# A fused dense-GELU forward and backward on one core: b2 of the first block by GpSimd, more waking products, one joined group of left-over products

## The chip, the cores and the metric

One core of a Trainium2 chip. The metric is the device time of one launch in microseconds (us). The engines are TensorE (PE in the profile: products, with PEld its weight loads), VectorE (DVE), ScalarE (ACT), GpSimd (POOL) and SyncE (SP, which here only issues DMAs).

## The reference

The forward pass of a dense layer with a tanh-approximated GELU, and its gradients for an incoming `grad_out`:

```python
def _fwd_reference(x, w1, b1, w2, b2):
    h = jnp.einsum("bsd,df->bsf", x, w1) + b1
    h = _gelu(h)
    return jnp.einsum("bsf,fd->bsd", h, w2) + b2
_out, _vjp = jax.vjp(_f, x, w1, b1, w2, b2)
_grads = _vjp(grad_out)
return (_out0, *[jnp.asarray(_g) for _g in _grads])
```

B = 1, S = 2048 rows, D = 448, F = 1792, everything bf16. Six outputs: out (out_0), and the gradients of x, w1, b1, w2 and b2 (out_1 to out_5).

## The kernel before

**Stages.** The rows are cut into four blocks of 512 (`SB`), F into 14 tiles of 128, taken in 7 pairs per block, so 28 pairs in all. For pair `f` of a block, TensorE forms u = x w1 (`pe_u_fulls`, `u_tail`), and for pair `k` q = grad_out w2^T (`pe_q_fulls`, `q_tail`). ScalarE copies u out with b1 added (`copy_u`), and makes gelu(u) (`act_gelu`, into hT), a square and a tanh; VectorE makes from those the derivative of the gelu (`dve_cubic`, `dve_gate`) and multiplies it with q (`dve_gh`, line 299, into ghT). From hT come the rows of out (a `Unit` of kind "o": 128 rows, 14 products with w2_sb), from ghT the rows of the gradient of x (kind "x", with w1T_sb). After all pairs follow the gradients of w1 (`gw1_full`, `gw1_tail`), of w2 (`gw2_tile`) and of the biases (`emit_sum`).

**Left-over products.** D = 448 is three tiles of 128 and a left-over of 64. The products of the three full tiles are the "fulls" (lines 212 and 258). The left-over has only 64 rows, half the array; `pe_tails(fs, ks)` issues those of u (line 227) and of q (line 234) in turn, u's in one half of the array and q's in the other, so that a u and a q run at the same time when both lists are given.

**Order.** The order of the instructions on every engine is written out by hand (`manual_schedule`); the waits between engines are added for the data and the buffers. The sequence in question is the start, lines 395 to 424: u of pair 0, copy, square, gelu; u of pair 1; u of pair 2 and its left-over; four units of block 0 are opened and given their first pair of products (`pieces(4, 0, -1)`); left-over and fulls of q of pair 0; the gate and gh of pair 0; another `pieces`. Then a loop over i = 1 to 7: u of pair i + 2, joined left-overs of u and q, q of pair i, tanh, the finished units' evictions around `copy_u`, gelu and square, VectorE's chain, and pieces of the open units. At i = 6 two units of kind "x" are opened, the first readers of w1T_sb. From pair 8 on, two pairs go through at a time. PSUM has four single banks (tags one0 to one3), which u and units share, and two double ones (two0, two1); up to q 7 all q's use two0, so the next q waits until gh has read the one before.

**Loads.** All first loads but one of w1's pieces are issued from SP one after another in the order of use: x in two transposing halves, pieces of w1 (w_f, with the left-over rows in wt), w2 (w_sb), grad_out transposed (gT), w2 transposed in pieces (w2T), b2 spread over the partitions (b_bc in the profile), x of the second block, the last of w2T, w1 transposed whole (w1T_sb), and grad_out of the second block. While x is on its way, TensorE runs 32 products of zeros, the waking products (line 172).

**Evictions.** A finished unit is copied from PSUM into one of five staging buffers (`st`) and stored by a DMA issued from GpSimd (line 342). Kind "x" is copied by ScalarE (line 339), kind "o" by VectorE, which adds b2 in the same instruction (line 341). The four "o" units of block 0 are an exception: b2 is added by a 15th product per unit, of `row0` (ones in its first row, zeros elsewhere) with b2_bc (line 332), and ScalarE copies them. In the last stages the same five `st` buffers hold the results of `gw1_full`, `gw1_tail` and `gw2_tile`; `gb2_w`, the row sum of grad_out, has a buffer of its own.

**Names.** The profile leaves numbers and some suffixes out of names: U, A, Z are U4, A4, Z4; row is row0; b_bc is b2_bc; w_sb is w2_sb.

Of the kernel before, what the change touches and what calls it, by code (L numbers as in the profile page):

```python
# [10 lines left out]
ALU = mybir.AluOpType  # L11
BF16 = mybir.dt.bfloat16
F32 = mybir.dt.float32
# [6 lines left out]
def kernel(  # L20
# [15 lines left out]
    nc = tc.nc  # L36
    P = 128
    B, S, D = x.shape
# [6 lines left out]
    SB = 512  # L45
    NB = S // SB
    SPB = SB // P
    NPAIR = NF // 2
    NSTEP = NB * NPAIR
    NSINGLE = 8  # L50
    LEAD = 2
    NWAKE = 32
    STG = 5
    ROW0 = [SB, 2 * SB, 3 * SB, 0]
    WIDE = (0, 1)
# [8 lines left out]
    const = ctx.enter_context(tc.tile_pool(name="const", bufs=1))  # L64
# [4 lines left out]
    stg = ctx.enter_context(tc.tile_pool(name="stg", bufs=STG))  # L69
# [6 lines left out]
    b1_t16 = const.tile([P, 32], BF16, name="b1_t16")  # L76
    b1T = const.tile([P, NF], F32, name="b1T")
    b2_bc = const.tile([P, D], BF16, name="b2_bc")
    row0 = const.tile([P, P], BF16, name="row0")
    w1_f = const.tile([P, KF, F], BF16, name="w1_f")  # L80
    w2T = const.tile([P, KF + 1, F], BF16, name="w2T")
    wt1 = const.tile([P, F], BF16, name="wt1")
# [9 lines left out]
    def two_banks(n, name):  # L92
        return psum.tile([P, 2, SB], F32, name=name, tag=f"two{n}")
# [40 lines left out]

    nc.vector.memset(zero[:], 0.0)
    nc.gpsimd.memset(b1_rows[:], 0.0)
    nc.vector.memset(row0[:], 0.0)
    nc.vector.memset(row0[0:1, :], 1.0)
    nc.gpsimd.dma_start(out=b1_rows[0:NF, :], in_=b1.rearrange("(ft p) -> ft p", p=P))
    xT[0] = blk.tile([P, KF + 1, SB], BF16, name="xT", tag="xT")  # L140
    halves = [slice(0, SB // 2), slice(SB // 2, SB)]
# [28 lines left out]
    pw = two_banks(1, "pw")  # L170
    for w in range(NWAKE):
        nc.tensor.matmul(pw[:, 0, 0:P], lhsT=zero[:], rhs=zero[:], start=True, stop=True)
# [30 lines left out]
    def pe_u_fulls(f):  # L203
        b, p = divmod(f, NPAIR)
        if p == 0:
            hT[b] = blk.tile([P, NF, SB], BF16, name="hT", tag="hT")
        banks = (2, 3) if f == 1 else (0, 1) if f < NSINGLE + LEAD else order_a[2 * (f % 2):2 * (f % 2) + 2]
        PU[f] = [one_bank(n, "pu") for n in banks]
        for rs in halves if f == 0 else [slice(0, SB)]:
            for a in range(2):  # L210
                for kt in range(KF):
                    nc.tensor.matmul(PU[f][a][:, rs], lhsT=w1_f[:, kt, cols(p, a)], rhs=xT[b][:, kt, rs],  # L212
                                     start=(kt == 0 and rs.start == 0), stop=False, skip_group_check=True)
# [4 lines left out]
    def open_q(k):  # L218
        b, p = divmod(k, NPAIR)
        if p == 0:  # L220
            ghT[b] = blk.tile([P, NF, SB], BF16, name="ghT", tag="ghT")
        PQ[k] = two_banks(0 if k < NSINGLE else order_b[k % 2], "pq")

    def u_tail(f, a):
        b, p = divmod(f, NPAIR)
        hf = half(b not in WIDE)
        nc.tensor.matmul(PU[f][a][:], lhsT=wt1[hf, cols(p, a)], rhs=xT[b][hf, KF, :], start=False, stop=True,  # L227
                         tile_position=(hf.start, 0), skip_group_check=True)

    def q_tail(k, a, swap=False):  # L230
        b, p = divmod(k, NPAIR)
        hf = half((b in WIDE) != swap)
        g = g_swap[b] if swap else gT[b][:, 0, :]
        nc.tensor.matmul(PQ[k][:, a, :], lhsT=w2T[hf, 0, cols(p, a)], rhs=g[hf, :], start=True, stop=False,  # L234
                         tile_position=(hf.start, 0), skip_group_check=True)

    def pe_tails(fs, ks):
        cross = bool(fs) and bool(ks) and (fs[0] // NPAIR in WIDE) != (ks[0] // NPAIR in WIDE)
        for k in ks:
            open_q(k)  # L240
        us = [(f, a) for f in fs for a in range(2)]
        qs = [(k, a) for k in ks for a in range(2)]
        if not us and len(ks) == 2:
            for a in range(2):
                q_tail(ks[0], a)
                q_tail(ks[1], a, swap=True)
            return
        for n in range(max(len(us), len(qs))):
            if n < len(us):
                u_tail(*us[n])  # L250
            if n < len(qs):
                q_tail(*qs[n], swap=cross)

    def pe_q_fulls(k):
        b, p = divmod(k, NPAIR)
        for a in range(2):
            for kt in range(1, KF + 1):
                nc.tensor.matmul(PQ[k][:, a, :], lhsT=w2T[:, kt, cols(p, a)], rhs=gT[b][:, kt, :], start=False, stop=(kt == KF),  # L258
                                 skip_group_check=True)
# [55 lines left out]
    class Unit:  # L315
        def __init__(self, kind, b, j):
            self.kind, self.b, self.j, self.done, self.ps = kind, b, j, 0, None
            self.b2_pe = kind == "o" and b == 0
            self.by_act = kind == "x" or self.b2_pe

        def avail(self, fmax, gmax):
            top = fmax if self.kind == "o" else gmax
# [2 lines left out]
        def emit(self, p):  # L325
            src, w = (hT, w2_sb) if self.kind == "o" else (ghT, w1T_sb)
            for a in range(2):
                nc.tensor.matmul(self.ps, lhsT=src[self.b][:, 2 * p + a, self.j * P:(self.j + 1) * P],  # L328
                                 rhs=w[:, 2 * FP[p] + a, :], start=(p == 0 and a == 0),
                                 stop=(p == NPAIR - 1 and a == 1 and not self.b2_pe), skip_group_check=True)  # L330
            if p == NPAIR - 1 and self.b2_pe:
                nc.tensor.matmul(self.ps, lhsT=row0[:], rhs=b2_bc[:], start=False, stop=True, skip_group_check=True)  # L332
            self.done += 1

        def evict(self):
            st = stg.tile([P, SB], BF16, name="st", tag="st")
            r = ROW0[self.b] + self.j * P
            if self.by_act:
                nc.scalar.copy(out=st[:, 0:D], in_=self.ps)  # L339
            else:  # L340
                nc.vector.tensor_tensor(out=st[:, 0:D], in0=self.ps, in1=b2_bc[:], op=ALU.add)
            nc.gpsimd.dma_start(out=(out2 if self.kind == "o" else gx2)[r:r + P, :], in_=st[:, 0:D])  # L342
# [16 lines left out]
    def open_two(n, units):  # L359
        t = two_banks(n, "ps")  # L360
        for h in range(units):
            open_unit(t[:, h, 0:D])

    def pieces(budget, fmax, gmax):
        for un in list(open_units):
            while un.done < un.avail(fmax, gmax) and budget > 0:
                un.emit(un.done)
                budget -= 1
            if un.done == NPAIR:
                open_units.remove(un)  # L370
                finished.append(un)
# [36 lines left out]
    act_square([1])  # L408
    act_gelu([1])
    pe_u_fulls(2)  # L410
    pe_tails([2], [])
    open_two(1, 2)
    for n in (2, 3):
        open_unit(one_bank(n, "ps")[:, 0:D])
    pieces(4, 0, -1)
    pe_tails([], [0])
    pe_q_fulls(0)
    dve_gate([0])
    dve_cubic([1])
# [86 lines left out]
    accg = blk.tile([P, D], F32, name="accg", tag="ghT")  # L506
# [30 lines left out]
    def emit_sum(n):  # L537
        for _ in range(n):
            if not sums:
                return  # L540
            kind, st_ = sums.pop(0)
            if kind == "g":
                in0 = g_nat[:, 0, :] if st_ == 1 else accg[:]
                nc.vector.tensor_tensor(out=accg[:], in0=in0, in1=g_nat[:, st_, :], op=ALU.add)
                if st_ == NS - 1:
                    gb2_w = stg.tile([P, D], BF16, name="gb2_w", tag="gb2", bufs=1)
                    nc.gpsimd.partition_all_reduce(gb2_w[:], accg[:], channels=P, reduce_op=bass_isa.ReduceOp.add)
                    nc.gpsimd.dma_start(out=out_5.rearrange("(o d) -> o d", o=1), in_=gb2_w[0:1, :])
            else:
                v = acc[:].rearrange("p (ft f) -> p ft f", f=P)  # L550
                b, j = PLACE[st_]
                in0 = gh_nat[:, PLACE[0][0], :, PLACE[0][1], :] if st_ == 1 else v
                nc.vector.tensor_tensor(out=v, in0=in0, in1=gh_nat[:, b, :, j, :], op=ALU.add)  # L553
                if st_ == NS - 1:
                    gb1_w = blk.tile([P, F], BF16, name="gb1_w", tag="ghT")
                    for c in range(4):
                        c0, c1 = c * 512, min(F, c * 512 + 512)
                        nc.gpsimd.partition_all_reduce(gb1_w[:, c0:c1], acc[:, c0:c1], channels=P, reduce_op=bass_isa.ReduceOp.add)
                    v1 = out_3.rearrange("(o f) -> o f", o=1)
                    nc.gpsimd.dma_start(out=v1[:, 2 * P:F], in_=gb1_w[0:1, 0:F - 2 * P])  # L560
                    nc.gpsimd.dma_start(out=v1[:, 0:2 * P], in_=gb1_w[0:1, F - 2 * P:F])
# [43 lines left out]
    for ft0, n in ((0, 4), (4, 4), (8, 4), (12, 2)):  # L605
        for kt in range(KF):
            gw1_full(ft0, n, kt)
            emit_sum(3)
        if ft0 == 4:
            gw1_tail(0, 4)  # L610
        if ft0 == 12:
            gw1_tail(8, 3)
# [35 lines left out]
```

## Time and profile before

| what | us |
|---|---|
| runs | 272.23, 274.29, 273.76 (median 273.76) |
| profiled execution | 273.81 |
| its span, first to last instruction | 272.0 |

| engine | busy us | share of the span |
|---|---|---|
| PE (TensorE) | 267.1 | 98% |
| DVE (VectorE) | 175.7 | 65% |
| ACT (ScalarE) | 139.4 | 51% |
| POOL (GpSimd) | 38.2 | 14% |

How to read the views: the page's slices cut the span into 40 parts of 6.8 us, and each digit is the busy share of a part in tenths. The chain of waits follows the work that ended last back from the last instruction; in order of time, each line is a start, a length and what it was, with xN for N instructions in a row. A product's time in the chain is what it adds to the one before. The timeline has a start, a length (from the first start to the last end of a group), engine, line, operation, tiles written and read, shape and count; SPq, ACTq and POOLq are the engines' issues of DMAs. A line of the DMA issues ends with the size or the number, and the us from issue to landing. All times count from the first instruction of the span.

### The profile page before, as it was taken

The page shows a single profiled execution, that of the slowest core. Times are in us where ns is not written, and L with a number is a line of the kernel's source. Part 1 is how long each engine was busy: PE and PEld are TensorE (multiplying, and loading weights), DVE is VectorE, ACT ScalarE, POOL GpSimd, SP SyncE. Part 2 cuts the span into 40 slices and gives each one's busy share as a digit, 9 for nine tenths or more (in the row PEclk, how much of TensorE's full clock was granted, in tenths as well). Part 3 has the DMA queues.
Part 4 walks back from the last instruction along what each step waited for, and adds up shares of the span by engine and source line. Part 5 has one row for each costly group of instructions (what it writes and reads, how often), then busy time and mean ns, then how long its engine had stood idle before and what let it go on. Part 6 is the DMA issues. An engine that isn't in the chain of part 4 may idle for free.

```text
span 272.0 us, 3706 instructions
## 1 busy us (share of the span) xinstructions
PE 267.1 (98%) x1434; PEld 129.6 (48%) x1434; DVE 175.7 (65%) x208; ACT 139.4 (51%) x163; POOL 38.2 (14%) x50
## 2 busy tenths in 40 slices
PE   7999999999999999999999999999999999999995
PEld 6334344444444445444454455554444485555554
DVE  1488999999989799685979931109999992000000
ACT  2699899799994678768668610011111121112111
POOL 1000003111001001010110102120520007900000
PEclk9999999999999999999999999999999999999999
DMA  7999989999999966194352549999111111999861
GB/s 164 221 200 216 184 171 189 289 250 199 260 225 241 236 171 154 34 190 83 106 115 85 111 97 289 378 215 217 39 40 38 41 39 31 194 225 222 206 125 34
DMA packets 112961, 44.37 MB, mean 163 GB/s; under 512 B 92032, under 2 KB 111824, under 8 KB 112944
## 3 DMA queue, kind: packets, MB, share of 16 engines
q1 hardware_dynamic: 106352, 36.43, 63.4%
q0 software_dynamic: 1824, 4.27, 4.9%
q10 hardware_dynamic: 4768, 3.44, 4.0%
q8 instruction: 11, 0.18, 0.3%
q14 instruction: 6, 0.05, 0.0%
HBM read 7.23 MB, written 14.23 MB: 79 GB/s over the span
## 4 chain that ended last, share of the span: by engine, by line
PE 97%; DMA 2%; ACT 0%; issue 0%
PE ps L328 31%; PE ps_v L599 16%; PE pq L258 14%; PE pu L212 14%; PE ps_w L567 13%; PE pu L227 5%; PE ps_w L578 2%; DMA xT<-in_x_dram 2%; PE pq L234 1%; PE ps L332 0%; ACT st L602 0%
## 5 line engine op out<-in xcount | busy, mean ns | idle before, releaser
L328 PE MATMUL ps<-w_sb,hT 128*128 128x448 bf16 x224 | 44.8, 352 | 0.0
L328 PE MATMUL ps<-w1T_sb,ghT 128*128 128x448 bf16 x224 | 43.8, 352 | 0.0
L267 ACT ACTIVATE U<-pu,b1T 128x512 bf16<-128x512 f32 x55 | 33.8, 686 | 19.2 <-PE pu L227 19.0
L599 PE MATMUL ps_v<-g_nat,h_nat 128*128 128x448 bf16 (+1 forms) x240 | 42.6, 340 | 0.0
L212 PE MATMUL pu<-xT,w_f 128*128 128x512 bf16 (+1 forms) x174 | 40.8, 383 | 0.8 <-DMA xT<-in_x_dram 0.8
L342 POOL DMA_DIRECT2D out_dram<-st x32 | 17.6, 551 | 163.4 <-ACT st L339 108.4
L258 PE MATMUL pq<-gT,w2T 128*128 128x512 bf16 x168 | 39.4, 380 | 0.0
L299 DVE SCALAR_TENSOR_TENSOR ghT<-Z,pq 128x1024 bf16<-128x1024 bf16 x28 | 33.8, 1220 | 7.6 <-PE pq L258 5.9
L567 PE MATMUL ps_w<-gh_nat,x_nat 128*128 128x512 bf16 (+1 forms) x192 | 36.7, 352 | 0.0
L285 ACT ACTIVATE Z<-Z 128x2048 bf16<-128x2048 bf16 (+1 forms) x18 | 27.5, 1528 | 10.2 <-DVE Z L281 9.9
L599 PEld LDWEIGHTS <-h_nat 128*128 128x128 bf16 x240 | 23.3, 98 | 19.3 <-issue 0.3
L328 PEld LDWEIGHTS <-hT 128*128 128x128 bf16 x224 | 21.8, 98 | 21.2 <-ACT U L267 0.4
L328 PEld LDWEIGHTS <-ghT 128*128 128x128 bf16 x224 | 21.9, 98 | 20.9
L553 DVE TENSOR_TENSOR acc<-acc,gh_nat 128x1792 f32<-128x1792 f32 x14 | 30.0, 2142 | 0.5
L276 ACT ACTIVATE A<-U 128x1024 bf16<-128x1024 bf16 (+1 forms) x19 | 27.7, 1456 | 0.9 <-DVE U L269 0.6
L273 ACT ACTIVATE hT<-U 128x1024 bf16<-128x1024 bf16 (+1 forms) x20 | 27.7, 1390 | 0.2
L212 PEld LDWEIGHTS <-w_f 128*128 128x128 bf16 x174 | 17.5, 101 | 20.8 <-issue 2.5
L567 PEld LDWEIGHTS <-x_nat 128*128 128x128 bf16 x192 | 18.7, 98 | 17.9 <-issue 0.4
L258 PEld LDWEIGHTS <-w2T 128*128 128x128 bf16 x168 | 15.0, 98 | 23.2 <-issue 7.6
L602 ACT CAST st<-ps_v 128x448 bf16<-128x448 f32 (+1 forms) x15 | 7.6, 507 | 34.8 <-PE ps_v L599 34.8
L339 ACT CAST st<-ps 128x448 bf16<-128x448 f32 x20 | 10.3, 529 | 27.7 <-PE ps L328 27.5
L570 ACT CAST st<-ps_w 128x512 bf16<-128x512 f32 (+1 forms) x12 | 6.4, 532 | 29.9 <-PE ps_w L567 29.9
(46 smaller groups left out, 197.3 us busy)
## 6 DMA issues: line engine op xcount, KB each, us to landing
hT_dram<-hT SPq DMA_DIRECT2D x28, 256.0 KB, 3.4
out_dram<-st POOLq DMA_DIRECT2D x32, 112.0 KB, 3.3
x_nat<-in_x_dram SPq DMA_DIRECT2D x1, 1792.0 KB, 11.3
g_nat<-in_grad_out_dram SPq DMA_DIRECT2D x1, 1792.0 KB, 16.4
out_dram<-st ACTq DMA_DIRECT2D x13, 112.0 KB, 3.4
w_f<-in_w_dram SPq DMA_DIRECT2D x6, 192.0 KB, 3.7
out_dram<-st ACTq DMA_DIRECT2D x9, 128.0 KB, 1.7
w_sb<-in_w_dram SPq DMA_DIRECT2D x5, 224.0 KB, 3.5
```

Of the source, the lines that this page charges most:

```text
L212: nc.tensor.matmul(PU[f][a][:, rs], lhsT=w1_f[:, kt, cols(p, a)], rhs=xT[b][:, kt, rs], start=(kt == 0 and rs.start == 0), stop=False, ski ...
L258: nc.tensor.matmul(PQ[k][:, a, :], lhsT=w2T[:, kt, cols(p, a)], rhs=gT[b][:, kt, :], start=False, stop=(kt == KF), skip_group_check=True)
L267: nc.scalar.activation(out=dst, in_=PU[f][a][:], func=ACT.Identity, bias=bias)
L273: nc.scalar.activation(out=rows(hT, r), in_=part(U4, r), func=ACT.Gelu_apprx_tanh)
L276: nc.scalar.activation(out=part(A4, ks), in_=part(U4, ks), func=ACT.Square, scale=math.sqrt(3.0 * GELU_A * GELU_C))
L285: nc.scalar.activation(out=z, in_=z, func=ACT.Tanh, scale=-1.0 / 3.0)
L299: nc.vector.scalar_tensor_tensor(out=rows(ghT, [k]), in0=part(Z4, [k]), scalar=1.0, in1=PQ[k][:], op0=ALU.add, op1=ALU.mult)
L328: nc.tensor.matmul(self.ps, lhsT=src[self.b][:, 2 * p + a, self.j * P:(self.j + 1) * P], rhs=w[:, 2 * FP[p] + a, :], start=(p == 0 and a = ...
L342: nc.gpsimd.dma_start(out=(out2 if self.kind == "o" else gx2)[r:r + P, :], in_=st[:, 0:D])
L553: nc.vector.tensor_tensor(out=v, in0=in0, in1=gh_nat[:, b, :, j, :], op=ALU.add)
L567: nc.tensor.matmul(ps[:, 0:n * P], lhsT=x_nat[:, st_, kt * P:(kt + 1) * P], rhs=gh_nat[:, b, ft0:ft0 + n, j, :], start=(st_ == 0), stop=(s ...
L599: nc.tensor.matmul(ps[:, 0:w], lhsT=h_nat[ft][:, st_, :], rhs=g_nat[:, st_, h * w:(h + 1) * w], start=(st_ == 0), stop=(st_ == NS - 1))
```

## The change

There are five edits. The number of waking products goes from 32 to 42. The four "o" units of block 0 lose their 15th product, and `row0` with its two clears goes; ScalarE copies such a unit into a new f32 buffer `wide_st` (two of them), and GpSimd adds b2_bc to it on the way into `st`, ahead of the store that it issues. The left-over products of the third u (pair 2) are no longer issued by themselves behind its fulls: they are joined with those of the first q, behind `pieces(4, 0, -1)`. `gb2_w` takes one of the five `st` buffers in place of its own.

```diff
-    NWAKE = 32
+    NWAKE = 42
...
-    row0 = const.tile([P, P], BF16, name="row0")
...
-    nc.vector.memset(row0[:], 0.0)
-    nc.vector.memset(row0[0:1, :], 1.0)
...
-            self.b2_pe = kind == "o" and b == 0
-            self.by_act = kind == "x" or self.b2_pe
+            self.b2_later = kind == "o" and b == 0
+            self.by_act = kind == "x" or self.b2_later
...
-                                 stop=(p == NPAIR - 1 and a == 1 and not self.b2_pe), skip_group_check=True)
-            if p == NPAIR - 1 and self.b2_pe:
-                nc.tensor.matmul(self.ps, lhsT=row0[:], rhs=b2_bc[:], start=False, stop=True, skip_group_check=True)
+                                 stop=(p == NPAIR - 1 and a == 1), skip_group_check=True)
...
-                nc.scalar.copy(out=st[:, 0:D], in_=self.ps)
+                if self.b2_later:
+                    wide_st = stg.tile([P, D], F32, name="wide_st", tag="wide_st", bufs=2)
+                    nc.scalar.copy(out=wide_st[:], in_=self.ps)
+                    nc.gpsimd.tensor_tensor(out=st[:, 0:D], in0=wide_st[:], in1=b2_bc[:], op=ALU.add)
+                else:
+                    nc.scalar.copy(out=st[:, 0:D], in_=self.ps)
...
     act_gelu([1])
     pe_u_fulls(2)
-    pe_tails([2], [])
     open_two(1, 2)
     for n in (2, 3):
         open_unit(one_bank(n, "ps")[:, 0:D])
     pieces(4, 0, -1)
-    pe_tails([], [0])
+    pe_tails([2], [0])
     pe_q_fulls(0)
...
-                    gb2_w = stg.tile([P, D], BF16, name="gb2_w", tag="gb2", bufs=1)
-                    nc.gpsimd.partition_all_reduce(gb2_w[:], accg[:], channels=P, reduce_op=bass_isa.ReduceOp.add)
+                    gb2_w = stg.tile([P, SB], BF16, name="st", tag="st")[:, 0:D]
+                    nc.gpsimd.partition_all_reduce(gb2_w, accg[:], channels=P, reduce_op=bass_isa.ReduceOp.add)
```

## The prediction

> **What bounds the kernel now.** The profile's page first, engines and slices:
>
> ```profile
> PE 267.1 (98%) x1434; PEld 129.6 (48%) x1434; DVE 175.7 (65%) x208; ACT 139.4 (51%) x163; POOL 38.2 (14%) x50
> PE   7999999999999999999999999999999999999995
> DVE  1488999999989799685979931109999992000000
> ```
>
> TensorE is busy from the first slice to the last, so any TensorE time that goes away counts, unless something else then makes it wait. VectorE is nearly full in slices 3 to 11 (14 to 75 us): there the second limit lies. All edits but one fall before 49 us. The chain of waits, in order of time, prices the start:
>
> ```profile
> 0.72 4.63 DMA xT<-in_x_dram
> 5.40 2.72 PE pu L212 x12
> 8.12 0.96 PE pu L227 x2
> 9.08 1.55 PE pu L212 x6
> 10.63 0.54 PE pu L227 x2
> 11.17 1.40 PE pu L212 x6
> 12.57 0.54 PE pu L227 x2
> 13.11 1.62 PE ps L328 x8
> 14.72 0.54 PE pq L234 x2
> ...
> 16.66 1.51 PE ps L328 x8
> 18.17 1.30 PE pu L212 x6
> ...
> 41.00 0.19 PE ps L332
> ```
>
> The first pair of left-over products took 0.96, later pairs 0.54; the first 12 half-width products 2.72, though six of full width take 1.30 to 1.40. So TensorE ran at about half pace until some 0.3 us into the piece at 9.08, about 9.4. Groups just behind left-over products take 0.11 more (1.62 against 1.51, 1.40 against 1.30). Last, the timeline and the DMA issues of 34 to 50 us:
>
> ```profile
> 34.73 6.35 SPq L167 DMA_TRANSPOSE w1T_sb<-in_w_dram  x1
> 37.36 1.22 DVE L299 SCALAR_TENSOR_TENSOR ghT<-Z,pq 128x1024 bf16<-128x1024 bf16 x1
> 38.64 0.37 PE L234 MATMUL pq<-gT,w2T 64*128 64x512 bf16 x1
> 42.54 1.22 DVE L299 SCALAR_TENSOR_TENSOR ghT<-Z,pq 128x1024 bf16<-128x1024 bf16 x1
> 45.97 2.81 PE L328 MATMUL ps<-w1T_sb,ghT 128*128 128x448 bf16 x14
> 47.72 1.22 DVE L299 SCALAR_TENSOR_TENSOR ghT<-Z,pq 128x1024 bf16<-128x1024 bf16 x1
> ```
>
> ```profile
> w1T_sb<-in_w_dram SPq DMA_TRANSPOSE x1, 10.6
> ```
>
> These carry the forecast. The load of w1T_sb lands at 34.73 + 10.6 = 45.33, and its first reader starts at 45.97. SP issues its loads one behind another and none of them waits for TensorE, so this landing does not come earlier when TensorE does.
>
> **Waking products.** The 32 of before run from 0.98 to 4.58, a row of 3.60, so (3.60 - 0.31)/31 = 0.106 apart (0.31 is one's length). Ten more add 1.06: the last starts at 5.32, x lands at 0.72 + 4.63 = 5.35, and the 0.83 us of idle before the first product is filled. Bounds: if they change nothing, the first product starts up to 0.1 later. If the unbroken work needed for full pace is what the trace shows, 5.40 to 9.4 (4.0 us), it is reached at 0.98 + 4.0 = 5.0, and the 4.0 us at half pace shrink by 2.0. I take 1.6, nearer the second: loads behind it hold TensorE too, the first q's w2T at 13.1 (issued at 9.32, 3.8 to landing; used at 14.66) and the third q's at 22.6 (15.38, 7.2; used at 24.15), margins of 1.6 and 1.5. ScalarE and VectorE begin on the first u and so shift with it.
>
> **Left-over products of the third u beside the first q's.** One group goes: its 0.54 and the 0.11 behind it, 0.65. The remaining group costs what joined groups already cost (19.47 to 20.01, 0.54). What the move delays is ScalarE's copy of the third u, at 15.86: TensorE would finish it at 12.57 + 8 x 0.19 + 0.54 = 14.63, so 1.2 us hide it; beyond them ScalarE and the gelu behind it are late one for one. VectorE idled 0.38 before the first gh, waiting for q, so of the 0.65 it can follow by 0.38.
>
> **b2 off TensorE.** Four products of 0.19: 0.76, between 41.0 and 42.9. The removed clears of row0 (VectorE at 0.88 and 1.07) end long before its next work at 5.18: nothing.
>
> **b2 on GpSimd.** Four adds of 128x448. ScalarE's copy keeps its row (0.53, 128x448 from PSUM); writing f32 in place of bf16 is bounded by 0.51 and 0.62, the shortest such copy and VectorE's eviction of that shape; I take 0.53, and the ends make 4 x 0.09 = 0.4 at most on an engine that idles 0.9 at 49.5. For the add the trace has two bounds: VectorE's running sum of the same shape and operand types (14 in 9.20, 0.66 each), and GpSimd's own all-reduce of that shape (4.58). I take 0.66, the same arithmetic, and keep the other for the range. Behind each add on GpSimd's queue stand its store and, behind the fourth, the two copies at 47.59 and 48.14, whose first reader is the mixed left-over group at 75: 20 us of cover. The third copy needs wide_st back: it starts at 45.70 and the first add can start at 43.5, so an add up to 2.2 us long makes nobody wait; a longer one holds ScalarE and the gelu, square and tanh behind it.
>
> Here the trace shows no instruction of GpSimd's arithmetic beside VectorE, so the price to VectorE lies between 0 and the whole adds. The slack first: the gh that the eighth q waits for ends at 48.94, the q's first product starts at 50.01. With VectorE 1.6 earlier and TensorE 0.6, that is 1.07 + 1.0 = 2.07. Three adds lie before that gh: 3 x 0.66 = 1.98, just hidden even if VectorE stands still for all of it. The Trainium skill, SBUF — State Buffer, "Who interferes with whom", speaks against the change: a GpSimd instruction that reads SBUF and a VectorE one with two SBUF inputs exclude each other for a whole instruction. No run here shows it yet. By its companion GPSIMD Engine Reference, section 3.1 (4497 ns for 2048 elements), an add would be 0.98, an estimate, and three would leave TensorE 0.9 late, 274.1 in all.
>
> **gb2_w in the st ring.** It is read by its store, issued at 198.52 and landed 2.1 later. The fifth later st copy, which gets its slot, starts at 218.45: 17.8 us of cover, cost nothing. Were it gone, ScalarE's copies and the two ps_w banks would wait for that landing.
>
> **The sum.** Removed before 45.97: 1.6 + 0.65 + 0.76 = 3.0 us of TensorE. It can't all be kept. VectorE's gh end at 38.58 (37.36 + 1.22) and 43.76; the sixth q already waited for the first (started at 38.64), and the seventh starts at 44.12, 0.36 behind the second. VectorE moves by 1.6, or by 0.38 if the pace stays; so TensorE reaches the seventh q at most 1.6 + 0.36 = 2.0 earlier (or 0.38 + 0.36 = 0.74). Either is more than what w1T_sb leaves: 45.97 - 45.33 = 0.64, less 0.05 from landing to start (5.35 to 5.40 for x), **0.6**. Behind it TensorE never waits in the trace of before, so 0.6 stays to the end. The profiled execution took 273.81 (span 272.0, 1.8 around it; the median is 273.76): 273.81 - 0.6 = **273.2**.
>
> **The rivals.**
> 1. *The load is no wall.* Outside a profile, or by chance, it lands earlier. For: one run of before took 272.23, 1.6 less than the profiled one, which a fixed landing would not allow from an early start alone. Against: landings of this queue keep to its issue times. Next in line is the second block's gT, 41.12 + 7.3 = 48.4 against its use at 50.01: 1.6. Time 273.8 - 1.6 = 272.2; chance 0.25.
> 2. *VectorE is held by the adds* (slower). It decides from 2.07/3 = 0.69 per add; the 0.6 is used up at 0.89. At twice VectorE's row (1.32) the eighth q waits 3.96 - 2.07 = 1.9: 275.1. For: VectorE has no idle time there. Against: the gh instructions (1.22 each) read q from PSUM and could cover some of it. Chance 0.17.
> 3. *The waking products don't raise the pace.* The sum above shows that this changes nothing at the end: TensorE is 0.74 ahead instead of 2.0, and the wall leaves 0.6. It is inside the forecast.
>
> **How the numbers follow.** Forecast 0.50 (its own range 272.8 to 273.6), rival 1 0.25, rival 2 0.17; 0.04 each are left for less than any of them and for adds near 4.58. The range takes the forecast, rival 1 with the scatter of a run below it, and the adds to about 1.15 each: 271.6 to 274.6. One per cent, 2.7 us, is about what a measurement of this kernel tells from no change. Under 271.0 would need more than the second wall allows, or a low draw: 0.11. Over 276.5 needs adds of 1.8 or more: 0.09. Within: 0.80.
>
> **What would show it.** No idle time between waking and pu; pairs of left-over products at 0.54 from the first or second; no lone group before 14; a TensorE wait of about 1 us at the first ps from w1T_sb, put down to that load, starting near 45.4. I am wrong if TensorE runs through there without a wait, or if it waits longer at the eighth q, behind gh.

## The result and the profile after

The changed kernel takes 274.9 us in the median of ten runs (274.6 to 275.51), the kernel before 273.73; the ratio is 1.0058, 95% interval 1.0039 to 1.0077. Its median is 1.2 us higher, where 0.6 less was forecast, and lies outside the range by 0.3. The ratio is not that of the medians: the runs of the kernel before fall into two groups, here four at 272.2 to 272.6 and six at 273.7 to 274.3, and its median lies in the upper one. One run of the kernel before (1580.48) and one of e4 (277.15) are left out of the ratios below as slow.

Its page, engines and TensorE's slices (span 273.7; this execution took 275.51, the longest of the ten; the others took 0.3 to 0.9 less, and what is shorter in them is not shown):

```profile
PE 265.6 (97%) x1440; PEld 129.2 (47%) x1440; DVE 179.7 (66%) x206; ACT 139.3 (51%) x163; POOL 44.2 (16%) x54
PE   7999998799999999999999999999999999999995
```

TensorE is busy 1.5 us less and the span is 1.7 longer: there is a dip in slices 7 and 8 (41 to 55 us) that was not there before. VectorE is busy 4.0 us longer, though it lost two clears and got no work. The start is as it was forecast but for the gap ahead of the first product: 0.6 us of wait for x are left of 0.83. The 42 waking products took only 3.95 (0.98 to 4.93), since their own pace rose on the way (314 ns each up to about 3.9, then 219), and x landed at 5.52. The chain of waits, start, length and what:

```profile
5.56 1.47 PE pu L209 x12
7.03 0.55 PE pu L224 x2
...
42.89 1.41 DVE Z L278
44.30 1.89 DVE A L286
...
46.94 1.17 DVE A L289
...
48.47 1.83 DVE Z L293
...
50.40 1.23 DVE ghT L296
51.63 0.04 issue
51.67 0.37 PE pq L231
```

The first products run at full pace, 1.47 in place of 2.72. But the chain that ends last runs over ScalarE and, from 21.74, over VectorE up to the eighth q at 51.67, which in the kernel before started at 50.01. TensorE's waits, with their total, number and longest:

```profile
PE pq L231 <- DVE ghT L296: 1.7, 1, 1.7
PE ps L325 <- DMA w1T_sb<-in_w_dram: 1.2, 1, 1.2
PE pw L169 <- DVE zero L134: 1.0, 1, 1.0
PE pu L209 <- DMA xT<-in_x_dram: 0.6, 1, 0.6
PE pq L231 <- DMA w2T<-in_w_dram: 0.5, 1, 0.5
```

The second is the wall of the forecast; the first is rival 2. Rows from the timeline of that stretch, VectorE, GpSimd and TensorE:

```profile
42.45 1.30 POOL L337 TENSOR_TENSOR st<-wide_st,b_bc 128x448 bf16<-128x448 f32 x1 [40.51 <-ACT wide_st L336]
42.89 1.41 DVE L278 TENSOR_TENSOR Z<-Z,U 128x1024 bf16<-128x1024 bf16 x1
44.06 0.74 POOL L342 DMA_DIRECT2D out_dram<-st  x1 [0.31 <-POOL st L337]
44.22 1.95 DVE L286 TENSOR_SCALAR A<-A 128x1024 bf16<-128x1024 bf16 x1
44.84 1.04 POOL L337 TENSOR_TENSOR st<-wide_st,b_bc 128x448 bf16<-128x448 f32 x1
45.54 2.82 PE L325 MATMUL ps<-w1T_sb,ghT 128*128 128x448 bf16 x14 [1.17 <-DMA w1T_sb<-in_w_dram]
46.76 1.05 POOL L337 TENSOR_TENSOR st<-wide_st,b_bc 128x448 bf16<-128x448 f32 x1
46.94 1.17 DVE L289 TENSOR_SCALAR A<-A 128x1024 bf16<-128x1024 bf16 x1
48.47 1.82 DVE L293 TENSOR_TENSOR Z<-Z,A 128x1024 bf16<-128x1024 bf16 x1
48.68 1.05 POOL L337 TENSOR_TENSOR st<-wide_st,b_bc 128x448 bf16<-128x448 f32 x1
49.59 0.39 PE L224 MATMUL pu<-xT,wt 64*128 64x512 bf16 x1
50.40 1.22 DVE L296 SCALAR_TENSOR_TENSOR ghT<-Z,pq 128x1024 bf16<-128x1024 bf16 x1
51.67 0.37 PE L231 MATMUL pq<-gT,w2T 64*128 64x512 bf16 x1 [1.70 <-DVE ghT L296]
```

The same four instructions of VectorE in the kernel before:

```profile
44.33 0.69 DVE L281 TENSOR_TENSOR Z<-Z,U 128x1024 bf16<-128x1024 bf16 x1
44.94 0.42 DVE L289 TENSOR_SCALAR A<-A 128x1024 bf16<-128x1024 bf16 x1
...
46.12 0.43 DVE L292 TENSOR_SCALAR A<-A 128x1024 bf16<-128x1024 bf16 x1
...
46.92 0.69 DVE L296 TENSOR_TENSOR Z<-Z,A 128x1024 bf16<-128x1024 bf16 x1
```

Beside each of the four adds stands one VectorE instruction that is stretched: 0.69 to 1.41, 0.42 to 1.95, 0.43 to 1.17, 0.69 to 1.82. That is 0.72 + 1.53 + 0.74 + 1.13 = 4.12 us more. VectorE's gh at 41.10 is 1.44 earlier than before (42.54); the next one, at 47.72 before, would have come at 46.28 and comes at 50.40, 4.12 later. TensorE's x products start at 45.54 against 45.97, 0.43 gained; at the eighth q it is 1.66 behind, and the span ends 1.7 later.

### The profile page after: what moved, and what is told of

Same layout as the page of the kernel before. It is cut to its first block, busy times and chain, and to the rows that moved or that the text cites. A ratio compares the mean times of both kernels' runs of the same rounds, so it can differ in the third digit from the quotient of the medians.

```text
span 273.7 us, 3726 instructions
## 1 busy us (share of the span) xinstructions
PE 265.6 (97%) x1440; PEld 129.2 (47%) x1440; DVE 179.7 (66%) x206; ACT 139.3 (51%) x163; POOL 44.2 (16%) x54
## 4 chain that ended last, share of the span: by engine, by line
PE 81%; DVE 11%; ACT 5%; DMA 2%; issue 1%; DVEq 0%; ACTq 0%
PE ps L325 26%; PE ps_v L598 16%; PE ps_w L566 13%; PE pq L255 10%; PE pu L209 9%; PE pu L224 3%; PE ps_w L577 2%; DVE ghT L296 2%; DMA xT<-in_x_dram 2%; DVE Z L293 2%; DVE Z L278 2%; ACT A L273 1%; ACT hT L270 1%; ACT U L264 1%; DVE A L288 1%; DVE A L286 1%
## 5 line engine op out<-in xcount | busy, mean ns | idle before, releaser
L209 PE MATMUL pu<-xT,w_f 128*128 128x512 bf16 (+1 forms) x174 | 39.4, 372 | 0.6 <-DMA xT<-in_x_dram 0.6
L342 POOL DMA_DIRECT2D out_dram<-st x32 | 19.1, 598 | 118.5 <-ACT st L339 63.4
L282 ACT ACTIVATE Z<-Z 128x2048 bf16<-128x2048 bf16 (+1 forms) x18 | 27.5, 1526 | 11.1 <-DVE Z L278 10.8
L209 PEld LDWEIGHTS <-w_f 128*128 128x128 bf16 x174 | 16.8, 98 | 19.5 <-issue 1.6
L339 ACT CAST st<-ps 128x448 bf16<-128x448 f32 x16 | 8.4, 529 | 28.3 <-PE ps L325 28.0
```

What stands on the lines that cost most here:

```text
L282: nc.scalar.activation(out=z, in_=z, func=ACT.Tanh, scale=-1.0 / 3.0)
```

## The experiments

Medians in us; ratios are to the kernel before in the same series, with 95% intervals. Since the median of before lies in the upper of its two groups, a kernel can have a lower median at a ratio of 1. Expectations speak of times against a median of 273.7 to 273.8 for the kernel before.

| kernel | median | ratio |
|---|---|---|
| changed kernel | 274.90 | 1.0058 (1.0039 to 1.0077) |
| e1: b2 by products | 273.06 | 0.9997 (0.9975 to 1.0019) |
| e2: no b2 | 272.82 | 0.9977 (0.9957 to 0.9997) |
| e7: four wide_st | 274.88 | 1.0057 (1.0036 to 1.0079) |
| e4: adds late | 273.54 | 1.0021 (0.9992 to 1.0050) |
| e3: adds only | 276.44 | 1.0136 (1.0103 to 1.0169) |
| e5: waking only | 273.55 | 1.0009 (0.9990 to 1.0028) |
| e6: joined group only | 273.47 | 0.9998 (0.9975 to 1.0021) |
| e8: e1, loads early | 272.80 | 0.9985 (0.9967 to 1.0003) |
| e9: b2 by VectorE | 273.49 | 0.9999 (0.9981 to 1.0017) |
| e10: e9, loads early | 273.35 | 1.0001 (0.9984 to 1.0017) |

**e1 and e2: take the adds away.** e1 puts the products back, e2 leaves b2 of the first 512 rows of out away altogether.

```diff
-                if self.b2_later:
-                    wide_st = stg.tile([P, D], F32, name="wide_st", tag="wide_st", bufs=2)
-                    nc.scalar.copy(out=wide_st[:], in_=self.ps)
-                    nc.gpsimd.tensor_tensor(out=st[:, 0:D], in0=wide_st[:], in1=b2_bc[:], op=ALU.add)
-                else:
-                    nc.scalar.copy(out=st[:, 0:D], in_=self.ps)
+                nc.scalar.copy(out=st[:, 0:D], in_=self.ps)
```

e1 has besides this the removed lines of `row0` and of line 332 again.

> The changed kernel with b2 of the first block back on TensorE (four products, ScalarE copies straight into st); the other edits stay. Theory A (GpSimd's adds hold VectorE, 4.1 us over four adds, and the eighth q waits 1.7 for gh): VectorE's four stretched instructions are back at 0.43 and 0.69, no wait at the eighth q, the wait for w1T_sb shrinks from 1.2 to about 0.8 because the products fill 0.4 of it, 273.2. Theory B (ScalarE's wait of 1.5 for wide_st makes gelu and square late, and VectorE behind them): the same 273.2. Theory C (the early start itself does harm later): about 274.9 as changed.

> The changed kernel without b2 in the first block's 512 rows of out: neither products nor adds (this part of the computation is left out). Theories A and B: 273.2 as e1, since the load of w1T_sb (lands at 45.5) is the wall for both, and TensorE waits 1.2 there. If the load is no wall outside a profile: 0.4 below e1. Theory C: 274.9.

Both lose the wait at the eighth q: their medians are 273.06 and 272.82, 1.8 and 2.1 below the changed kernel. So theory C falls: an early start does no harm by itself. TensorE's waits in e2:

```profile
PE pw L169 <- DVE zero L134: 1.0, 1, 1.0
PE ps L325 <- DMA w1T_sb<-in_w_dram: 0.8, 1, 0.8
```

The wall is there in e2 (0.8) and missing in e1, whose w1T_sb landed (33.77 + 11.1 = 44.9) just before its reader started at 44.91. This pair doesn't separate A from B, since it takes away ScalarE's wait too.

**e7: the adds without ScalarE's wait.** In the changed kernel ScalarE waited 1.5 for wide_st, the rival explanation.

```diff
-                    wide_st = stg.tile([P, D], F32, name="wide_st", tag="wide_st", bufs=2)
+                    wide_st = stg.tile([P, D], BF16, name="wide_st", tag="wide_st", bufs=4)
```

> The changed kernel with four wide_st in bf16 in place of two in f32, so that ScalarE's third and fourth copy wait for no add; the adds stay where they are. Theory A: VectorE is stretched by about 4 us all the same and the eighth q waits about 1.7: 274.9. Theory B: no late gelu or square, no wait at the eighth q: 273.2.

274.88, as slow as the changed kernel, with no wait of ScalarE for an add left in its profile. TensorE's longest wait in e7:

```profile
PE pq L231 <- DVE ghT L296: 2.3, 1, 2.3
```

Theory B falls. VectorE's instructions beside the adds in e7:

```profile
42.59 0.82 DVE L277 TENSOR_SCALAR Z<-A 128x1024 bf16<-128x1024 bf16 x1
...
44.06 1.50 DVE L286 TENSOR_SCALAR A<-A 128x1024 bf16<-128x1024 bf16 x1
...
46.32 1.17 DVE L289 TENSOR_SCALAR A<-A 128x1024 bf16<-128x1024 bf16 x1
...
47.86 1.81 DVE L293 TENSOR_TENSOR Z<-Z,A 128x1024 bf16<-128x1024 bf16 x1
```

They are stretched by 0.39 + 1.08 + 0.74 + 1.12 = 3.33, with bf16 inputs as with f32 ones.

**e4: the same adds where nobody waits for VectorE.** As e7, with the adds and their stores issued later, two at a time.

```diff
...
+                    held.append((wide_st, r))
+                    return
...
+    def add_held(n):
+        for wide_st, r in held[:n]:
+            st = stg.tile([P, SB], BF16, name="st", tag="st")
+            nc.gpsimd.tensor_tensor(out=st[:, 0:D], in0=wide_st[:], in1=b2_bc[:], op=ALU.add)
+            nc.gpsimd.dma_start(out=out2[r:r + P, :], in_=st[:, 0:D])
+        del held[:n]
...
+            if n in (4, 5):
+                add_held(2)
             pieces(28, k + 1, k - 1)
```

> As e7, but the four adds and their stores are issued two at a time in the fifth and sixth pair of pairs (about 96 to 115 us), where VectorE had 2.5 us without work before a gh and TensorE needs that gh later. Theory A: the adds stretch VectorE there by about as much, but nothing waits for it, and the eighth q no longer waits: 273.2. If GpSimd's adds cost TensorE time wherever they are: 274.9.

273.54, 1.4 below the changed kernel and not told apart from the kernel before: the wait at the eighth q is gone, though the adds still stretch VectorE. Ten of its twelve runs lie between 272.9 and 275.0; two took 276.94 and 277.15, both with a mean granted clock of 0.994 (the granted clock is the share of its full clock that the profile shows for TensorE; the others have 0.998 to 1.0). The profile is of a run of 274.00, so what made those two long stays open. The timeline of e4 shows which instructions are stretched (lines of GpSimd, then of VectorE):

```profile
106.80 1.62 POOL L349 TENSOR_TENSOR st<-wide_st,b_bc 128x448 bf16<-128x448 bf16 x1 [7.02 <-issue]
...
109.50 1.04 POOL L349 TENSOR_TENSOR st<-wide_st,b_bc 128x448 bf16<-128x448 bf16 x1
...
112.48 1.04 POOL L349 TENSOR_TENSOR st<-wide_st,b_bc 128x448 bf16<-128x448 bf16 x1
...
114.40 1.04 POOL L349 TENSOR_TENSOR st<-wide_st,b_bc 128x448 bf16<-128x448 bf16 x1
```

```profile
107.57 1.41 DVE L289 TENSOR_SCALAR A<-A 128x2048 bf16<-128x2048 bf16 x1
108.90 2.20 DVE L292 TENSOR_SCALAR Z<-Z 128x2048 bf16<-128x2048 bf16 x1
111.14 1.23 DVE L293 TENSOR_TENSOR Z<-Z,A 128x2048 bf16<-128x2048 bf16 x1
112.58 2.52 DVE L296 SCALAR_TENSOR_TENSOR ghT<-Z,pq 128x1024 bf16<-128x1024 bf16 x2 [0.21 <-PE pq L255]
```

Beside the first two adds the two TENSOR_SCALAR, 0.69 and 0.68 without an add, take 1.41 and 2.20. Beside the last two run the two gh instructions, one input from PSUM, and they keep their 2.52. The long add at 106.80 began while a VectorE instruction between SBUF tensors ran (106.31 to 107.54), which kept its own 1.23; there it was the add that took 0.6 longer. So the adds hold VectorE's work between SBUF tensors, and not gh.

**e3, e5, e6: one part of the change alone on the kernel before.** e3 moves b2 to GpSimd (with `row0` gone and gb2_w in the st ring), e5 `NWAKE = 42`, e6 the moved `pe_tails`.

> The kernel before with only b2 moved to GpSimd (row0 and its products gone, gb2_w in the st ring); 32 waking products, the third u's left-overs by themselves. Theory A (GpSimd's adds hold VectorE): VectorE's gh for the eighth q, at 48.9 before, ends 3.3 to 4.1 later, and the eighth q, wanted at about 49.6, waits 2.6 to 3.4; the products give back 0.4 to 0.8: 275.8 to 276.8. If the adds only harm where TensorE starts early: 273.4 to 273.8.

> The kernel before with 42 waking products and nothing else. TensorE at full pace from about 5.5 and about 1.6 earlier up to 45; TensorE waits for w1T_sb about 0.9 there, and 0.6 stays: 273.2. If the runs of before near 272.3 and near 273.9 differ by the moment at which the pace rises, all runs of this kernel lie close together. If the waking products don't raise the pace: 273.8 and two clusters.

> The kernel before with the third u's left-over products joined to the first q's and nothing else. One group of 0.65 goes from TensorE; VectorE can follow by the 0.38 that it waited for the first q: about 273.4, with the same scatter as before. If VectorE's later pace takes it all: 273.8.

e3: 276.44, 2.7 above before and 1.5 above the whole change, in the range of theory A. Without the earlier start VectorE's slack is smaller, and the eighth q waits 2.5 in the profile, which is of the longest of six runs (278.56). After it comes something that I had not expected, and that theory A's sum did not contain; that the median fits it is in part luck. The windows of e3 (busy time of PE, PEld, DVE, ACT and POOL, then the granted clock):

```profile
50.00:53.00 3.00, 0.58 (x3) 0.10 (x2) 2.90 (x2) 1.30 (x2) 2.68 (x5) 1.00 1.12 283
53.00:58.00 5.00, 4.93 (x17) 1.92 (x17) 4.65 (x9) 2.69 (x3) 0.05 (x1) 0.66 1.08 217
```

In the 5 us behind the wait the granted clock is 0.66. The x products there take 4.19 for 14, against 2.82, and the six of q ahead of them 1.82, against 1.47: 1.7 lost. At half pace for a share s, 1 - s/2 = 0.66 gives s = 0.68, 3.4 us, which costs the same 1.7. All six runs have a mean clock of 0.992 to 0.994, so they share this loss; e7, with 2.3 of wait, has 0.998 to 1.0. The Trainium skill, TensorE: Matmul & The Clock Gate, Part 1, has the clock set by how busy TensorE was in windows of 3.4 us, halved after an idle one. The 3.4 us agree, but here one wait of 2.5 was enough.

e5 and e6 can't be told from no change: their medians are 0.2 and 0.3 below that of before, where 0.6 and 0.3 were expected. The kernel before is itself no single time: of 28 runs in this series 14 lie between 272.2 and 273.3 and 14 between 273.7 and 274.2. e6's profile, with 32 waking products, took 272.39 and begins like this:

```profile
0.98 3.50 PE L172 MATMUL pw<-zero 128*128 128x128 bf16 x32 [0.98 <-DVE zero L135]
5.70 1.47 PE L212 MATMUL pu<-xT,w_f 128*128 128x256 bf16 x12 [1.22 <-DMA xT<-in_x_dram]
```

Full pace from the first product, in spite of 1.2 us of idle time ahead of it. Up to here e6 has the instructions of the kernel before, so the moment at which the pace rises differs with the same instructions. With 42 waking products (e5) the runs didn't close up either: 8 of 12 lie between 273.2 and 274.0, one at 272.3, three at 274.4 to 274.5. Why they aren't all low stays open; the profile of e5 (274.49) shows 1.7 of wait for w1T_sb, which landed late there, 34.93 + 11.7 = 46.6, so TensorE's early pace was lost again at that wall.

**e8: the wall moved.** e1, with w2's last two pieces and b2 issued from ScalarE's queue in the loop, one per iteration, in place of SP's.

```diff
-    load_w2(nc.sync, 12, NF)
-    load_w2(nc.sync, 0, 2)
...
+        if i == 1:
+            load_w2(nc.scalar, 12, NF)
+        if i == 2:
+            load_w2(nc.scalar, 0, 2)
...
```

> As e1 (all edits but GpSimd's adds), and the last two pieces of w2 and b2 are issued from ScalarE's queue in the loop in place of SP's, so that SP issues w1T_sb and the second block's gT 1.7 us earlier. If w1T_sb's landing is what caps the gain: it lands near 43.2, TensorE doesn't wait for it, 272.6 and up to 0.5 below e1. If VectorE's gh chain is the cap (e1 had no wait for w1T_sb): as e1, 273.1.

272.80; its profile shows no wait for w1T_sb. It is the fastest that computes all outputs, 2.1 below the changed kernel, but its interval against the kernel before (0.9967 to 1.0003) just holds no change, and e1's overlaps with it.

**e9 and e10: VectorE adds b2 itself.** `by_act` is `kind == "x"` alone, so the first block is evicted by line 341's instruction as the others are; e10 has e8's loads too.

> The changed kernel, but VectorE evicts the first block's four units and adds b2 in the same instruction, as it does in the other blocks (0.62 each in the profile of before); no wide_st, no add on GpSimd. If GpSimd's adds cost VectorE their whole length (3.3 to 4.1 us in the runs so far), doing the work itself costs it less, 4 x 0.55 to 0.62 = 2.2 to 2.5 ahead of the eighth q's gh, and that q waits 0.0 to 0.5 in place of 1.7 to 2.3: 273.0 to 273.4. If what held VectorE was the eviction work itself, whoever does it: 274.9.

> As e9, with w2's last two pieces and b2 issued from ScalarE's queue as in e8, so that w1T_sb lands about 1.5 earlier. TensorE then reaches the eighth q earlier and VectorE is the bound there: the gain at w1T_sb is given back at the eighth q, 272.9 to 273.3, no better than e9 by more than 0.3, and e8 (272.8) stays the fastest.

In e9 the four evictions, and what is late behind them:

```profile
42.59 2.21 DVE L336 TENSOR_TENSOR st<-ps,b_bc 128x448 bf16<-128x448 f32 x4
```

```profile
PE pq L231 <- DVE ghT L296: 0.8, 1, 0.8
```

Doing the whole eviction costs VectorE 2.21, while being beside GpSimd's adds cost it 3.3 to 4.1 and left ScalarE's copies to be made besides. The wait is 0.8, over the 0.5 that I allowed, and the median 273.49, a little over the expected 273.4. e10 waits as long (0.8), and its median is 0.1 lower, less than the noise: VectorE is the bound there, as expected.

## Why the prediction was wrong

- **What failed** is the size of one term: b2 on GpSimd, "3 x 0.66 = 1.98, just hidden even if VectorE stands still for all of it". The slack stood beside it as 2.07 and came out so, with some luck: VectorE was 1.44 earlier in place of 1.6, TensorE 0.42 in place of 0.6. TensorE reached the eighth q's left-overs at 49.59, and gh without the adds would have ended at 46.28 + 1.22 = 47.50: 2.09. The adds took 1.30, 1.04, 1.05 and 1.05, not VectorE's 0.66, and four, not three, came ahead of that gh, because the held gh itself got later. Three adds of the measured lengths, 3.39, would by the same sum have made 1.3 of delay, 274.5, still inside the range. VectorE lost 4.12; 4.12 - 2.09 = 2.03 is the delay from 49.59 to 51.67 but for the start of a product. The nearest row was that of another engine. The estimate of 0.98, worked out from a figure of the Trainium skill's GPSIMD Engine Reference (section 3.1), was nearer: with it and four adds the sum would have been 1.9 of delay. That estimate and this trace agree within 0.1 for three of the four adds.
- **That VectorE stands still** was left open between 0 and all of it. e7 shows it (3.33 of 4.2 us of adds), and e4 that gh doesn't take part. The rule that was quoted against the change (the Trainium skill, SBUF — State Buffer, "Who interferes with whom") agrees with what the two instructions of two SBUF inputs did (0.69 to 1.41 and to 1.82). VectorE's TENSOR_SCALAR, one SBUF input, were held as well, which the same section has for the modes that use a second port; the profile doesn't show the mode.
- **Rival 2** named this mechanism, this q and the point from which it decides (0.69 per add), its time at 1.32 per add was 275.1, and the wait at the eighth q was the sign of being wrong. It had a chance of 0.17. Its counterweight, that gh could cover some of it, was true only where gh and add happened to meet.
- **Waking products**: full pace from the first product (1.47 for 12), and VectorE 1.44 earlier against 1.6, as forecast. In seven of the other eight profiles with 42 waking products the first twelve took 1.57 to 1.97; in e4 x came in two steps. But what they are worth was reckoned against one execution of before; e6, with 32, reached full pace early too.
- **The joined group** is there, and its q waits 0.5 for w2T, as the margins at 13.1 had it. Alone (e6) its gain wasn't resolved.
- **The products of b2** were not worth 0.76 at the end: e2, without them, waits 0.8 at w1T_sb, where e1, with them, does not wait, and the medians differ by 0.2.
- **The wall at w1T_sb** was right as a mechanism: TensorE waited 1.2 for it and started at 45.54. Without the adds the forecast's 273.2 stands between e1 and e2's 272.8 to 273.1 and e4's 273.5. Rival 1's 272.2 was not reached, even in e8, which does not wait for that load (272.8). What was wrong is that the landing is fixed and keeps to the issue. In profiles with SP's first loads in the same order it came at 33.52 + 9.4 = 42.9 (e3), 45.33 (before), 45.5 (changed) and 46.6 (e5).
- **Staging**: no wait for gb2_w's slot shows in the changed kernel's profile, and its one wait for an st buffer (2.1, VectorE) stands in that of before too (2.08). ScalarE's wait of 1.5 for wide_st did happen, though adds up to 2.2 were to make nobody wait: that counted the third copy at 45.70, but it came at 43.84, and the fourth waited for the second add, which had the first add's store ahead of it. e7 shows that this cost nothing.

## What to carry to other kernels

An add that is moved to GpSimd is not off VectorE's hands: in these runs VectorE's work between SBUF tensors stood still beside it, 3.3 to 4.1 us for four adds, more than the 2.2 that VectorE needs to do the evictions itself. Before moving work off a full engine, look at which engine is the second limit at that place, and count the slack to the next one who waits for it; the same adds, some 60 us later, left TensorE no wait behind gh. And price an instruction by the engine that runs it: the row of another engine, 0.66, was here a lower bound, not a middle.

## What the runs showed of the hardware

- TensorE's pace rises at moments that differ between runs of the same instructions: at about 9.4 us in the profile of before, ahead of 5.7 in e6's, with the same 32 waking products; with 42, at about 3.9 in the changed kernel's, only behind the last waking product in e1's (they take 4.66 there, 3.95 in the changed kernel). The runs of before span 2.4 us (271.96 to 274.39). The changed kernel's ten lie within 0.9; in its profile the chain runs over ScalarE and VectorE to the eighth q, so the landing of w1T_sb does not set its end there.
- One wait of 2.5 us in mid-kernel brought the granted clock to 0.66 over the next 5 us (e3), a second loss of about 1.7; with 2.3 of wait (e7) the clock stayed at 1.0 over the 11 us behind it, and with 1.7 (the changed kernel) too.
- GpSimd's add of 128x448 takes 1.03 to 1.05 in most cases, and as long with bf16 inputs as with f32. The two longer ones, 1.30 in the changed kernel and 1.62 in e4, began while a VectorE instruction between SBUF tensors ran.
- In the changed kernel the TENSOR_SCALAR at 44.22 was held already 0.6 ahead of the second add's row, while GpSimd issued a store (44.06 to 44.80). Such an issue beside VectorE's work in the profile of before (43.78 to 44.96) stretched nothing, nor did those in e2 (44.38 to 45.60), so I take it that the add holds VectorE from a little before its row starts; no run separates the two.
